# Attention with a learned bias and a gated MLP on one core: the bias hidden layer without a scale per row, and one more rounding on ScalarE

## The chip, the core and the metric

One core of a Trainium2 chip. The metric is the device time of one execution in microseconds (us). The time before is the median of three runs.

## The reference

Two stages, float32 in and out: attention over 4 batches, 8 heads, 576 positions and 64 columns a head, with a bias that a small network makes from the distance of two positions, and then an MLP of 512 to 2048 to 512 with the gate h * sigmoid(1.702 h).

```python
scores = scale * np.matmul(q, k.transpose(0, 1, 3, 2))
psi_rel = np.log1p(np.abs(rel))                                  # rel = i - j
psi_i = np.log1p(np.maximum(pos[:, None].astype(np.float32), 1.0))
x = (psi_rel / psi_i)[..., None]
h = np.maximum(x @ w1 + b1, 0.0)                                 # 32 hidden units
bias = h @ w2                                                    # 8 heads
scores = scores + bias.transpose(2, 0, 1)[None, :, :, :]
...
h = x @ w_in
g = h * (1.0 / (1.0 + np.exp(-1.702 * h)))
return (g @ w_out).astype(np.float32)
```

## The kernel before, in words

The queries are cut into five chunks of positions: four of 128 and one of 64. A unit is one batch, one chunk and one pair of heads. There are 72 units. For each, TensorE makes the scores (line 349), VectorE adds the bias and finds the row's extreme (L365), ScalarE takes the exponential and its sum (L369), and the probabilities are written as a rounded half-precision part (L381 on ScalarE, L379 on VectorE) and the rest of it (L382 on VectorE). A transposing DMA on SyncE's queue (L391) turns them, TensorE multiplies them with the values (L414), and VectorE writes the result as a high and a low half-precision part (L419, L420).

When the units of two batches in one chunk are done, they form a block of the MLP, of 256 tokens (128 for the last chunk). A block has 16 steps. In one step TensorE makes 128 hidden columns (L492), ScalarE takes the tanh (L498), VectorE makes the gate (L500), the gate is rounded to half precision (L505 on ScalarE for the blocks named in `ACT_G`, L507 on VectorE for the others), GpSimd takes the difference (L508), and TensorE multiplies high and low part with the second weight matrix two steps later (L522, `LAG = 2`). Both weight matrices come in 32 pieces; each is put together and split by four operations on VectorE (L456, L459, L462, L218) and one on ScalarE (L468).

The bias does not depend on the batch. It is made once, in 36 steps of 16 rows each, chunk by chunk (`bias_step`, or `bias_hidden` and `bias_products` as two halves). The 128 partitions hold four rows of 32 hidden units. `tab` holds the logarithm of the distance, 4 phases of 288 entries, and a window of 4 x 144 entries of it is the distance of 4 rows from all 576 columns. One step has four relus (line 163 on ScalarE or line 165 on VectorE, by the letters in `BIAS_ENG`: three on VectorE and one on ScalarE for each of the first 8 steps, all four on ScalarE in the next 16, two and two in the last 12), eight products on TensorE (L183, L185) into one PSUM buffer, an eviction on ScalarE (L189) and a store to a scratch tensor in DRAM (L190). The units load it from there (L204). The first 8 steps stand before the first unit, the others lie among the units.

The relus before multiply the window by `sc`, which is w1 divided by the logarithm of the row, with a scale for each partition. On ScalarE the bias b1 is added in the same operation. On VectorE the operation is a multiplication and a maximum with -b1, and the missing b1 times w2 is added where the products leave PSUM: `oc` holds this for each number of ScalarE relus in a step.

The library that builds the program orders the instructions of each engine itself: it goes by the order in which they are written as a priority, and by a planner's estimate of when each can start. Every engine then takes its own instructions strictly in that order.

Of the kernel before, what the change touches and what calls it, by code (L numbers as in the profile page):

```python
# [7 lines left out]
F32 = mybir.dt.float32  # L8
F16 = mybir.dt.float16
U32 = mybir.dt.uint32  # L10
ACTF = mybir.ActivationFunctionType
ALU = mybir.AluOpType
# [3 lines left out]
LPH = 288  # L16
PB0 = 144
# [3 lines left out]
def kernel(  # L21
# [26 lines left out]
    nc = tc.nc  # L48
    B, H, S, D = q.shape
# [22 lines left out]
    VEC_EXP = {u: 1 for u in (*range(33, 42), *range(62, 72))}  # L72
    VEC_EXP.update({u: 2 for u in (5, 6, 42, *range(54, 62))})
    POOL_W = set()
    ACT_G = {4, 6, 9}


    W_AHEAD = 3
# [7 lines left out]
    cst = ctx.enter_context(tc.tile_pool(name="cst", bufs=1))  # L86
# [9 lines left out]
    tab = cst.tile([128, 4, LPH], F32, name="tab")  # L96
    pk = cst.tile([128, 178], F32, name="pk")
    sc, w2b, w1c, b1c = pk[:, 0:144], pk[:, 144:176], pk[:, 176:177], pk[:, 177:178]
    b1n = cst.tile([128, 1], F32, name="b1n")
    oc = cst.tile([128, 5], F32, name="oc")  # L100
    scr = [dr.tile([128 if c < 4 else ST, H, S], F32, name=f"scr{c}") for c in range(5)]


# [15 lines left out]
    for g in range(B // 2):  # L119
        b0, b1_ = 2 * g, 2 * g + 1  # L120
        for c in range(5):
            n = 128 if c < 4 else ST
# [6 lines left out]


    def bias_setup():
        nc.scalar.activation(out=oc[:, 4:5], in_=oc[:, 4:5], func=ACTF.Relu)
        nc.vector.tensor_scalar(out=b1n, in0=b1c, scalar1=-1.0, scalar2=None, op0=ALU.mult)
        nc.vector.tensor_scalar(out=sc, in0=sc, scalar1=w1c, scalar2=None, op0=ALU.mult)
        nc.vector.tensor_scalar(out=w2b, in0=w2b, scalar1=BS, scalar2=None, op0=ALU.mult)
        p = ps_h.tile([128, 512], F32, tag="h", name="pc")
        for r in range(4):
            nc.tensor.matmul(p[32 * r:32 * r + 32, 0:1], lhsT=w2b, rhs=b1c, start=True, stop=True)
        for na in range(4):
            n = 32 * (4 - na)  # L140
            nc.vector.tensor_copy(oc[:n, na:na + 1], p[:n, 0:1])

    def bias_step(c, s, eng, htags, ostag):

        bias_products(c, s, eng, bias_hidden(c, s, eng, htags), ostag)

    def bias_hidden(c, s, eng, htags):
        hts = []
        na = eng.count("A")
        assert eng.endswith("A" * na)
        for r in range(4):
            if r % 2 == 0:
                ht = stage([128, 2, S], F32, htags[r // 2], "ht")
                hts.append(ht)
            h = ht[:, r % 2, :].rearrange("k (c p) -> k c p", c=4)
            pb, col = 32 * c + 4 * s + r, 32 * c + 4 * s + r  # L160
            tv = tab[:, :, PB0 - pb:PB0 - pb + 144]
            if eng[r] == "A":
                nc.scalar.activation(out=h, in_=tv, func=ACTF.Relu, bias=b1c, scale=sc[:, col:col + 1])  # L163
            else:
                nc.vector.tensor_scalar(  # L165
                    out=h, in0=tv, scalar1=sc[:, col:col + 1], scalar2=b1n, op0=ALU.mult, op1=ALU.max
                )
        return hts

    def bias_products(c, s, eng, hts, ostag):  # L170
        na = eng.count("A")
        where = BIAS_PSUM.get(8 * c + s)
        if where is None:
            o = ps_s.tile([128, 4, 512], F32, tag="s", name="o")[:, 0:2].rearrange("p a n -> p (a n)")
        else:
            o = ps_o.tile([128, 2, 512], F32, tag="o", name="o").rearrange("p a n -> p (a n)")
        om, ot = o[:, 0:SM], o[:, SM:S]
        for x in range(2):
            for r in range(4):
                h = hts[r // 2][:, r % 2, :].rearrange("k (c p) -> k c p", c=4)  # L180
                po = slice(32 * r, 32 * r + 32)
                if x == 0:
                    nc.tensor.matmul(om[po], lhsT=w2b, rhs=h[:, :, 0:128], start=True, stop=True)  # L183
                else:
                    nc.tensor.matmul(  # L185
                        ot[po], lhsT=w2b, rhs=h[:, :, 128:144].rearrange("k c p -> k p c"), start=True, stop=True
                    )
        os_ = wk.tile([128, S], F32, tag=ostag, name="os", bufs=BUFS[ostag])
        nc.scalar.activation(out=os_, in_=o[:, 0:S], func=ACTF.Identity, bias=oc[:, na:na + 1])  # L189
        nc.scalar.dma_start(out=scr[c][16 * s:16 * s + 16].rearrange("p h n -> (p h) n"), in_=os_)  # L190

    bt_t = {}
# [18 lines left out]
    def stage(shape, dt, tag, name):  # L211
        return wk.tile(shape, dt, tag=tag, name=name, bufs=BUFS[tag])
# [268 lines left out]
    def emit_m1(j, f):  # L481
# [21 lines left out]
        gt = wk.tile([128, 2, 256], F16, tag="gT", name="gT", bufs=BUFS["gT"])  # L503
        if j in ACT_G:
            nc.scalar.copy(gt[:, 0, :n], g[:, :n])  # L505
# [74 lines left out]
    for g in range(B // 2):  # L580
        b0, b1_ = 2 * g, 2 * g + 1
        o = g * UPG
# [15 lines left out]
            ):  # L598
                at(o + u, *x)

    nc.gpsimd.memset(oc, 0.0)
    nc.sync.dma_start(out=tab, in_=dist.rearrange("p (f a) -> p f a", a=LPH))
    nc.scalar.dma_start(out=pk, in_=pack)
    load_k(0, 0, "a32")
# [8 lines left out]
        out=idn, in_=idn, compare_op=ALU.not_equal, fill=1.0, base=0, pattern=[[-1, 128]], channel_multiplier=1  # L613
    )
    bias_setup()
    load_v(1, 0)
    load_k(0, 1)
    HT0 = ("ht", "hl", "ht", "aT")
    for s in range(8):
        bias_step(0, s, BIAS_ENG[s], (HT0[(2 * s) % 4], HT0[(2 * s + 1) % 4]), ("os", "bt")[s // 2 % 2])  # L620
        if s in FIRST:
            FIRST[s][0](*FIRST[s][1:])
    for x in SECOND:
        x[0](*x[1:])
    bq = [(c, i) for c in range(1, 5) for i in range(8 if c < 4 else 4)]
# [4 lines left out]
    def bias_first():  # L630
        if bq:
            c, i = bq.pop(0)
            eng = BIAS_ENG[8 * c + i]
            half.append((c, i, eng, bias_hidden(c, i, eng, ("ht", "ht"))))

    def bias_second():
        if half:
            x = half.pop(0)
            bias_products(*x, "os")
            bdone[x[0]] += 1  # L640
# [98 lines left out]
```

## Time and profile before

| | |
|---|---|
| median of 3 runs (lowest, highest) | 725.68 us (724.52, 728.96) |
| the profiled execution | 725.27 us, of which 723.5 us are the span from the first to the last instruction |
| TensorE matmul busy | 642.0 us, 89% of the span |
| VectorE busy | 514.7 us, 71% |
| ScalarE busy | 408.1 us, 56% |
| GpSimd busy | 133.9 us, 19% |
| mean granted TensorE clock | 0.959 of full speed |

The busy times are unions over the whole span. The span has two very different parts, and the shares of the whole describe neither. In the rows below PE is TensorE's matmul, PEld its weight load, DVE VectorE, ACT ScalarE, POOL GpSimd, and SPq, ACTq the instruction queues of SyncE and ScalarE. A number after L is a line of the kernel before. An operation's duration and the step from its start to the next one's start are not the same: neighbours on one engine overlap by some 0.1 us.

### The profile page before, as it was taken

What the parts mean: (1) busy time and instruction counts of PE and PEld (TensorE: products, weight loads), DVE (VectorE), ACT (ScalarE), POOL (GpSimd) and SP (SyncE); (2) the same over time, 40 slices, a digit from 0 to 9 for tenths busy, and PEclk for the clock granted to TensorE, in tenths of its full rate; (3) what the DMA queues carried; (4) which work ended last, traced back from release to release, by engine and by line L of the source; (5) the groups of instructions that cost most, each with busy time, mean ns of one, the idle gap of its engine ahead of it and who ended that gap; (6) DMA issues with size and microseconds to landing.
All of it is one profiled execution on the core that took longest, in us unless ns stands there. A gap on an engine that the chain in (4) does not pass through costs nothing. (4 is left out here: it accounts for less than half of the span.)

```text
span 723.5 us, 17516 instructions
## 1 busy us (share of the span) xinstructions
PE 642.0 (89%) x6888; PEld 385.0 (53%) x6888; DVE 514.7 (71%) x1416; ACT 408.1 (56%) x847; POOL 133.9 (19%) x194
## 2 busy tenths in 40 slices
PE   5655777869969999999979899899999999999997
PEld 3212333425536655656646465566666666666765
DVE  6865998798957766777677877855775896775321
ACT  6897978686558655665544446743443453343133
POOL 1202000111201111212221112121222222212222
PEclk9967978998989999999999999999999999999999
DMA  9889999968997656867576789955564475745000
GB/s 241 236 259 237 240 241 289 259 158 221 216 175 174 132 116 134 178 149 154 127 173 115 164 146 148 189 134 107 100 129 106 100 167 126 122 77 96 2 31 15
DMA packets 230771, 111.80 MB, mean 155 GB/s; under 512 B 210720, under 2 KB 214944, under 8 KB 230688
## 3 DMA queue, kind: packets, MB, share of 16 engines
q1 hardware_dynamic: 222592, 94.65, 62.7%
q10 hardware_dynamic: 7952, 15.43, 7.0%
q8 instruction: 54, 0.88, 0.5%
q0 software_dynamic: 144, 0.59, 0.2%
q14 instruction: 29, 0.24, 0.1%
HBM read 52.85 MB, written 15.34 MB: 94 GB/s over the span
## 5 line engine op out<-in xcount | busy, mean ns | idle before, releaser
L492 PE MATMUL hp<-xT,wi 128*128 128x256 f16 (+1 forms) x1920 | 216.9, 265 | 4.5 <-DVE th L500 3.6
L522 PE MATMUL op<-wo,gT 128*128 128x512 f16 x864 | 214.4, 381 | 4.9 <-DVE sm L376 2.4
L508 POOL TENSOR_TENSOR gT<-th,gT 128x256 f16<-128x256 f32 (+1 forms) x160 | 118.5, 742 | 513.0 <-DVE gT L507 279.9
L492 PEld LDWEIGHTS <-wi 128*128 128x128 f16 x1920 | 168.0, 98 | 48.5 <-issue 15.7
L369 ACT ACTIVATE a<-a,mx 128x576 f32<-128x576 f32 x144 | 110.4, 767 | 107.2 <-DVE mx L365 104.5
L382 DVE SCALAR_TENSOR_TENSOR hl<-a,sm,hl 128x576 f16<-128x576 f32 x144 | 121.7, 854 | 16.9 <-ACT hl L381 16.6
L365 DVE CUSTOM_DVE_ANT_0 a<-sp,bt 128x576 f32<-128x576 f32 x144 | 103.0, 752 | 35.5 <-PE sp L349 30.5
L522 PEld LDWEIGHTS <-gT 128*128 128x128 f16 x864 | 78.9, 98 | 84.1 <-POOL gT L508 5.1
L498 ACT ACTIVATE th<-hp 128x256 f32<-128x256 f32 (+1 forms) x160 | 56.4, 353 | 114.6 <-PE hp L492 109.6
L500 DVE SCALAR_TENSOR_TENSOR th<-th,hp 128x256 f32<-128x256 f32 (+1 forms) x160 | 62.2, 390 | 76.2 <-ACT th L498 76.0
L414 PE MATMUL ot<-aT,v 128*64 128x128 f16 (+1 forms) x2280 | 79.5, 221 | 26.8 <-DMA aT<-hl 25.2
L414 PEld LDWEIGHTS <-v 128*64 128x64 f16 x2400 | 69.5, 114 | 63.2 <-issue 43.1
L381 ACT ACTIVATE hl<-a,sm 128x576 f16<-128x576 f32 x103 | 76.3, 766 | 30.0 <-DVE sm L377 11.9
L183 PE MATMUL o<-ht,pk 128*32 128x512 f32 x288 | 69.6, 690 | 17.2 <-ACT os L189 13.8
L163 ACT ACTIVATE ht<-tab,pk 128x576 f32<-128x576 f32 x96 | 78.3, 860 | 9.3 <-PE o L185 5.0
L349 PE MATMUL sp<-kT,qT 64*128 64x512 f16 (+2 forms) x960 | 72.1, 292 | 8.2 <-DVE mx L365 5.9
L349 PEld LDWEIGHTS <-qT 64*128 64x128 f16 (+1 forms) x960 | 29.6, 98 | 56.9 <-issue 26.9
L419 DVE TENSOR_SCALAR xT<-ot 128x128 f16<-128x128 f32 x72 | 20.4, 284 | 22.1 <-PE ot L414 21.8
L507 DVE CAST gT<-th 128x256 f16<-128x256 f32 x112 | 32.6, 291 | 3.5
L376 DVE TENSOR_SCALAR sm<-sm 128x1 f32<-128x1 f32 x144 | 21.0, 149 | 16.2 <-ACT a L369 15.5
L189 ACT ACTIVATE os<-o,oc 128x576 f32<-128x576 f32 x36 | 26.3, 730 | 10.2 <-PE o L185 9.4
L165 DVE TENSOR_SCALAR ht<-tab,pk,b1n 128x576 f32<-128x576 f32 x48 | 26.9, 609 | 4.9 <-PE o L185 4.9
(57 smaller groups left out, 416.3 us busy)
## 6 DMA issues: line engine op xcount, KB each, us to landing
bt<-scr SPq DMA_DIRECT2D x31, 576.0 KB, 4.6
scr<-os ACTq DMA_DIRECT2D x36, 288.0 KB, 5.0
w<-in_moe_w_in_dram SPq DMA_DIRECT2D x16, 512.0 KB, 5.1
w<-in_moe_w_out_dram SPq DMA_DIRECT2D x16, 512.0 KB, 5.6
k<-in_k_dram SPq DMA_DIRECT2D x32, 128.0 KB, 3.9
q<-in_q_dram SPq DMA_DIRECT2D x16, 256.0 KB, 4.6
out_dram<-ob ACTq DMA_DIRECT2D x16, 256.0 KB, 3.0
bt<-scr SPq DMA_DIRECT2D x8, 288.0 KB, 4.1
```

The lines of the kernel that those rows point to most:

```text
L163: nc.scalar.activation(out=h, in_=tv, func=ACTF.Relu, bias=b1c, scale=sc[:, col:col + 1])
L183: nc.tensor.matmul(om[po], lhsT=w2b, rhs=h[:, :, 0:128], start=True, stop=True)
L349: nc.tensor.matmul(ps[a][64 * e:64 * e + m, cs], lhsT=qt[r, x, hp + e, 0:m], rhs=kT[b, hp + e][r, y, cs], start=i == 0, stop=i == 2,)
L365: nc.vector.tensor_tensor_reduce(out=at[:, cs], in0=s_ps.pop((u, a))[:, 0:S], in1=bt[:, cs], scale=-1.0 / BS, scalar=3.0e38, op0=ALU.add, ...
L369: nc.scalar.activation(out=at[:, cs], in_=at[:, cs], func=ACTF.Exp, scale=-1.0, bias=mx[:, a:a + 1], accum_out=sm[:, a:a + 1],)
L381: nc.scalar.activation(out=hl[:, 0, cs], in_=at[:, cs], func=ACTF.Identity, scale=r)
L382: nc.vector.scalar_tensor_tensor(out=hl[:, 1, cs], in0=at[:, cs], scalar=r, in1=hl[:, 0, cs], op0=ALU.mult, op1=ALU.subtract)
L414: nc.tensor.matmul(o[64 * a:64 * a + 64, po], lhsT=vt[:, x, vc:vc + 64], rhs=t[:, 9 * y + k0, po], start=kb < 0 and i == 0, stop=kb == 3 a ...
L492: nc.tensor.matmul(p[:, :n], lhsT=wi16[:, x, cc, 128 * f:128 * f + 128], rhs=r, start=i == 0, stop=i == 11,)
L500: nc.vector.scalar_tensor_tensor(out=g[:, :n], in0=th[:, :n], scalar=1.0, in1=p[:, :n], op0=ALU.add, op1=ALU.mult)
L508: nc.gpsimd.tensor_tensor(out=gt[:, 1, :n], in0=g[:, :n], in1=gt[:, 0, :n], op=ALU.subtract)
L522: nc.tensor.matmul(op_t[j, i], lhsT=gt[:, x, ts], rhs=wo16[:, f, y, :], start=f == 0 and n3 == 0, stop=f == NF - 1 and n3 == 2,)
```

## The change

The relus no longer multiply. The table is multiplied by w1 once, in place, and the bias of a row becomes b1 times the logarithm of the row (`bp`). As the logarithm is not negative, the relu of this is the old hidden value times that logarithm, and the division by it is done at the eviction with a scale for each partition (`ips`). A ScalarE relu has one per-partition operand (the bias) where it had two, a VectorE relu adds one per-partition operand and takes the maximum with a constant, where it had two per-partition operands. The eviction has a scale where it had a bias.

The setup is done in two parts by the new function `bias_scale`: what the first 8 steps need (32 columns of `bp`, table entries 112 to 287) before them, and the rest (112 columns, entries 0 to 111) after the last relus of these steps on their engines. `ips` is made by four products of the packed table with a matrix of ones (`one`, five small writes by GpSimd) and one copy. Besides this, `ACT_G` gets block 0, so the 16 gate roundings of the first MLP block move from VectorE (L507) to ScalarE (L505).

```diff
-    ACT_G = {4, 6, 9}
+    ACT_G = {0, 4, 6, 9}
...
     def bias_setup():
-        nc.scalar.activation(out=oc[:, 4:5], in_=oc[:, 4:5], func=ACTF.Relu)
-        nc.vector.tensor_scalar(out=b1n, in0=b1c, scalar1=-1.0, scalar2=None, op0=ALU.mult)
-        nc.vector.tensor_scalar(out=sc, in0=sc, scalar1=w1c, scalar2=None, op0=ALU.mult)
+        nc.scalar.activation(out=ips[:, 0:1], in_=one[:, 0:1], func=ACTF.Relu)
+        bias_scale(slice(0, 32), slice(PB0 - 32, LPH))
         nc.vector.tensor_scalar(out=w2b, in0=w2b, scalar1=BS, scalar2=None, op0=ALU.mult)
         p = ps_h.tile([128, 512], F32, tag="h", name="pc")
         for r in range(4):
-            nc.tensor.matmul(p[32 * r:32 * r + 32, 0:1], lhsT=w2b, rhs=b1c, start=True, stop=True)
-        for na in range(4):
-            n = 32 * (4 - na)
-            nc.vector.tensor_copy(oc[:n, na:na + 1], p[:n, 0:1])
+            nc.tensor.matmul(
+                p[32 * r:32 * r + 32, 0:36], lhsT=one, rhs=sc.rearrange("k (x r) -> k x r", r=4)[:, :, r],
+                start=True, stop=True,
+            )
+        nc.vector.tensor_copy(ips, p[:, 0:36])
+
+    def bias_scale(rows, dist):
+        nc.vector.reciprocal(out=bp[:, rows], in_=sc[:, rows])
+        nc.scalar.activation(out=tab[:, 2:4, dist], in_=tab[:, 2:4, dist], func=ACTF.Copy, scale=w1c)
+        nc.vector.tensor_scalar(out=bp[:, rows], in0=bp[:, rows], scalar1=b1c, scalar2=None, op0=ALU.mult)
+        nc.vector.tensor_scalar(
+            out=tab[:, 0:2, dist], in0=tab[:, 0:2, dist], scalar1=w1c, scalar2=None, op0=ALU.mult
+        )
...
             if eng[r] == "A":
-                nc.scalar.activation(out=h, in_=tv, func=ACTF.Relu, bias=b1c, scale=sc[:, col:col + 1])
+                last["A"] = nc.scalar.activation(out=h, in_=tv, func=ACTF.Relu, bias=bp[:, pb:pb + 1])
             else:
-                nc.vector.tensor_scalar(
-                    out=h, in0=tv, scalar1=sc[:, col:col + 1], scalar2=b1n, op0=ALU.mult, op1=ALU.max
+                last["V"] = nc.vector.tensor_scalar(
+                    out=h, in0=tv, scalar1=bp[:, pb:pb + 1], scalar2=0.0, op0=ALU.add, op1=ALU.max
                 )
...
-        nc.scalar.activation(out=os_, in_=o[:, 0:S], func=ACTF.Identity, bias=oc[:, na:na + 1])
+        nc.scalar.activation(out=os_, in_=o[:, 0:S], func=ACTF.Copy, scale=ips[:, 8 * c + s:8 * c + s + 1])
...
-    nc.gpsimd.memset(oc, 0.0)
+    nc.gpsimd.memset(one, 0.0)
+    for r in range(4):
+        nc.gpsimd.memset(one[32 * r:32 * r + 1, 8 * r:8 * r + 8], 1.0)
...
+    with tc.issue_after(last["V"].ins), tc.issue_after(last["A"].ins):
+        bias_scale(slice(32, 144), slice(0, PB0 - 32))
     for x in SECOND:
         x[0](*x[1:])
```

## Rows read from the trace of the kernel before

**Rows 1.** Busy time by stretch; columns: stretch, length, PE, PEld, DVE, ACT, POOL, clock, DMA, GB/s.

```profile
0.00:36.00 36.00, 21.35 (x203) 11.08 (x204) 25.89 (x52) 26.90 (x42) 8.32 (x21) 1.00 0.96 238
36.00:126.00 90.00, 61.73 (x542) 24.98 (x542) 72.34 (x186) 77.98 (x136) 4.71 (x5) 0.79 1.01 255
126.00:160.00 34.00, 28.46 (x255) 13.90 (x253) 28.50 (x67) 26.17 (x46) 6.81 (x6) 1.00 0.85 206
160.00:215.00 55.00, 41.91 (x422) 24.78 (x422) 45.48 (x117) 32.47 (x63) 7.62 (x8) 0.89 0.98 211
215.00:330.00 115.00, 112.98 (x1230) 68.11 (x1228) 84.48 (x242) 71.66 (x144) 19.86 (x27) 0.99 0.67 145
```

**Rows 2.** Waits of the first 135 us: who for whom, total us, times, longest us.

```profile
PE o L183 <- ACT os L189: 13.8, 9, 4.2
...
PE ot L414 <- DMA aT<-hl: 7.6, 3, 5.2
...
DVE a L365 <- DMA bt<-scr: 4.4, 2, 3.9
...
DVE wo L218 <- ACT wo L468: 3.2, 1, 3.2
```

**Rows 3.** Groups by line and shape: busy us, mean ns of one, idle before, releasers.

```profile
L163 ACT ACTIVATE ht<-tab,pk 128x576 f32<-128x576 f32 x96 | 78.3, 860 | 9.3 <-PE o L185 5.0 <-DVE pk L134 2.8 <-ACT ht L163 0.7
L381 ACT ACTIVATE hl<-a,sm 128x576 f16<-128x576 f32 x103 | 76.3, 766 | 30.0 <-DVE sm L377 11.9 <-issue 10.2 <-DMA aT<-hl 3.6
L165 DVE TENSOR_SCALAR ht<-tab,pk,b1n 128x576 f32<-128x576 f32 x48 | 26.9, 609 | 4.9 <-PE o L185 4.9
L189 ACT ACTIVATE os<-o,oc 128x576 f32<-128x576 f32 x36 | 26.3, 730 | 10.2 <-PE o L185 9.4 <-DMA out_dram<-ob 0.5
L507 DVE CAST gT<-th 128x256 f16<-128x256 f32 x112 | 32.6, 291 | 3.5
L377 DVE RECIPROCAL sm<-sm 128x1 f32<-128x1 f32 x144 | 21.9, 158 | 2.1
L379 DVE TENSOR_SCALAR hl<-a,sm 128x576 f16<-128x576 f32 x41 | 21.4, 527 | 0.7 <-DMA aT<-hl 0.2
L505 ACT CAST gT<-th 128x256 f16<-128x256 f32 x16 | 6.4, 397 | 4.1 <-DVE th L500 4.1
L134 DVE TENSOR_SCALAR pk<-pk 128x144 f32<-128x144 f32 x1 | 0.3, 285 | 0.0
```

**Rows 4.** Timeline, first 41 us: start, duration, what, idle before it and its releaser.

```profile
5.06 0.15 DVE L133 TENSOR_SCALAR b1n<-pk 128x1 f32<-128x1 f32 x1 [5.06 <-DMA pk<-in_pack_dram]
...
5.45 3.16 ACT L163 ACTIVATE ht<-tab,pk 128x576 f32<-128x576 f32 x4 [2.76 <-DVE pk L134]
...
14.57 1.56 DVE L165 TENSOR_SCALAR ht<-tab,pk,b1n 128x576 f32<-128x576 f32 x3 [1.92 <-PE o L185]
...
24.48 0.68 DVE L218 SCALAR_TENSOR_TENSOR qT<-qp,qT 128x512 f16<-128x512 f32 x1
...
29.48 0.72 ACT L189 ACTIVATE os<-o,oc 128x576 f32<-128x576 f32 x1
...
40.81 0.76 DVE L365 CUSTOM_DVE_ANT_0 a<-sp,bt 128x576 f32<-128x576 f32 x1 [3.93 <-DMA bt<-scr]
```

**Rows 5.** Stretches of line 163 alone: length, ACT busy and count, clock, DMA.

```profile
36.00:126.00 90.00, 34.65 (x43) 0.79 1.01 255
126.00:160.00 34.00, 13.08 (x16) 1.00 0.85 206
```

**Rows 6.** Stretches of line 507 alone: length, DVE busy and count, clock, DMA.

```profile
126.00:160.00 34.00, 1.71 (x6) 1.00 0.85 206
160.00:215.00 55.00, 2.22 (x8) 0.89 0.98 211
```

**Rows 7.** TensorE's timeline from 75 us, the product with the turned probabilities.

```profile
163.84 1.81 PE L414 MATMUL ot<-aT,v 128*64 128x128 f16 x30 [4.14 <-DMA aT<-hl]
```

**Rows 8.** Waits from 196 to 216 us, who for whom, total us, times, longest us.

```profile
PE ot L414 <- DMA aT<-hl: 5.6, 1, 5.6
```

More of the change, by code (lines that the diff above doesn't have):

```diff
@@ L98 @@
     sc, w2b, w1c, b1c = pk[:, 0:144], pk[:, 144:176], pk[:, 176:177], pk[:, 177:178]
-    b1n = cst.tile([128, 1], F32, name="b1n")
-    oc = cst.tile([128, 5], F32, name="oc")
+    bp = cst.tile([128, 144], F32, name="bp")
+    ips = cst.tile([128, 36], F32, name="ips")
+    one = cst.tile([128, 32], F32, name="one")
     scr = [dr.tile([128 if c < 4 else ST, H, S], F32, name=f"scr{c}") for c in range(5)]
@@ L137, in bias_setup @@
         for r in range(4):
-            nc.tensor.matmul(p[32 * r:32 * r + 32, 0:1], lhsT=w2b, rhs=b1c, start=True, stop=True)
-        for na in range(4):
-            n = 32 * (4 - na)
-            nc.vector.tensor_copy(oc[:n, na:na + 1], p[:n, 0:1])
+            nc.tensor.matmul(
[10 more added lines that the diff above has]
+        )
+    last = {}
     def bias_step(c, s, eng, htags, ostag):
@@ L152, in bias_hidden @@
         hts = []
-        na = eng.count("A")
-        assert eng.endswith("A" * na)
         for r in range(4):
@@ L159, in bias_hidden @@
             h = ht[:, r % 2, :].rearrange("k (c p) -> k c p", c=4)
-            pb, col = 32 * c + 4 * s + r, 32 * c + 4 * s + r
+            pb = 32 * c + 4 * s + r
             tv = tab[:, :, PB0 - pb:PB0 - pb + 144]
             if eng[r] == "A":
-                nc.scalar.activation(out=h, in_=tv, func=ACTF.Relu, bias=b1c, scale=sc[:, col:col + 1])
+                last["A"] = nc.scalar.activation(out=h, in_=tv, func=ACTF.Relu, bias=bp[:, pb:pb + 1])
             else:
-                nc.vector.tensor_scalar(
-                    out=h, in0=tv, scalar1=sc[:, col:col + 1], scalar2=b1n, op0=ALU.mult, op1=ALU.max
+                last["V"] = nc.vector.tensor_scalar(
+                    out=h, in0=tv, scalar1=bp[:, pb:pb + 1], scalar2=0.0, op0=ALU.add, op1=ALU.max
                 )
@@ L170, in bias_products @@
     def bias_products(c, s, eng, hts, ostag):
-        na = eng.count("A")
         where = BIAS_PSUM.get(8 * c + s)
```

## The prediction

> **What bounds the kernel now.** I read the busy times by stretch first [rows 1], since the whole says only that TensorE is busy for 642 of 723.5 us. From 215 to 330 us TensorE is busy for 112.98 of 115 us at a clock of 0.99, and the slices after it stay like that. What is saved on another engine there is hidden. The first 215 us are the part that can give: TensorE works for 21.35 + 61.73 + 28.46 + 41.91 = 153 us of them and is idle for 62. Between 36 and 126 us the two engines that carry the change are nearly full, VectorE with 72.34 and ScalarE with 77.98 of 90 us, the DMA engines show a share of 1.01, and the mean granted clock is 0.79, so part of it ran at 2.4 GHz and part at the lower level, with TensorE idle for 28 us in between. From 126 to 215 us VectorE has 28.50 + 45.48 = 74.0 of 89 us and ScalarE 58.6.
>
> Next come the waits, to see who is late in that part [rows 2]. TensorE waits 13.8 us for the eviction of the bias products (one PSUM buffer takes turns, so a product waits for ScalarE's eviction of the step before), and in single pieces of up to 5.2 us for transposed probabilities. VectorE waits 4.4 us for the bias loads and 3.2 us for ScalarE's part of a weight piece. TensorE's other two large holes are of the same kind, 4.14 us before the product at 163.84 [rows 7] and 5.6 us before the one at 211.6 [rows 8], both ended by a transposing DMA. So this part is a relay of VectorE, the SyncE queue with its transposes, and ScalarE. ScalarE is the fullest for 90 us, but it is rarely the last to arrive.
>
> **What one operation gives.** The groups by shape [rows 3] hold the same ScalarE form with one per-partition operand and with two, on 576 columns each: 766 ns at L381 and 860 ns at L163. The relu loses one operand, so I take 860 - 766 = 94 ns off each. On VectorE L379 has one such operand and takes 527 ns, L165 has two and takes 609 ns, so 82 ns go. L379 writes half precision and L165 does not, which makes this the weaker of the two. In all, 96 x 94 = 9.0 us of ScalarE and 48 x 82 = 3.9 us of VectorE. The evictions have one operand before and after and count as nothing, at most the 730 - 766 = 36 ns either way that separate two forms with one operand, 1.3 us over 36 off the path.
>
> **Part by part, against the profiled execution of 725.27 us** (2 us more than its span, and 0.41 us under the median of the three runs, which is inside their spread).
>
> Start, 0.3 us later. The packed inputs arrive at 5.06 us and the first relus start at 5.45 us on both engines [rows 4]. Now the table has to be multiplied in between: 352 columns on either engine. For 576 columns and one per-partition operand ScalarE takes 766 ns [rows 3]. If that were all proportional, 352 columns would take 766 x 352 / 576 = 468 ns, and if none of it were, 766, so I take about 0.6 us. The table is then ready near 5.7 us. The bound below is -0.6 us (the 8 relus that VectorE runs first give back 0.7 us and nothing else comes later), above +0.6.
>
> The first 8 steps, nothing. VectorE runs ahead by the two buffers and then waits 1.92 us for the products to let go of them [rows 4], so its 24 faster relus (2.0 us) end in a longer wait. The ScalarE relus save 8 x 94 ns = 0.75 us where it waits too.
>
> Second part of the setup, 0.7 us later. It stands in the program ahead of the query transposes of the second batch, on VectorE behind the last relu of step 7. In this trace the subtraction of that transpose starts there at 24.48 us [rows 4]. Queued behind the new operations are that subtraction, then the key transposes on TensorE, the products of step 7, the eviction at 29.48 us, its store, and the bias load that ends VectorE's wait of 3.93 us at 40.81 us. Two multiplications cost about 285 ns (L134, 144 columns) and between 285 and 527 ns for 224 columns, so 0.33. The reciprocal of 112 columns shows only its one-column time, 158 ns, in this trace. The bound above is the 285 ns of a 144-column operation from the rows, doubled for a slower operation. That is 0.75 to 1.2 us in durations, some 0.2 less in starts, and I take 0.7. Below it is 0, if the planner puts the subtraction first, above 1.2.
>
> The reciprocal is the one operation whose growth with the columns no row shows, since all 144 of them have one column and take 158 ns [rows 3]. The Trainium skill, VectorE: DVE Perf Modes, section First, the fixed hardware budget, says that a reciprocal is an iterated division with a repeat count of 8. An estimate from that page, 8 cycles a column at 0.96 GHz, is 0.93 us for the 112 columns, and the sum would be 0.7 us higher by it.
>
> ScalarE relus among the units, 0.8 us earlier. Between 36 and 126 us there are 43 of them and 16 more up to 160 us [rows 5]. 59 x 94 ns = 5.5 us is the most. Of the waits of other engines in the first 135 us, 13.8 us on the evictions and 3.2 us on a weight part end on ScalarE [rows 2], against a stretch of about 100 us with units in it. That is one us in six, and 5.5 / 6 = 0.9, of which I take 0.8. Below the bound is -5.5, above 0.
>
> The gate roundings of block 0, 1.5 us earlier. Fourteen of the 16 lie between 126 and 215 us [rows 6]. VectorE loses 16 x 291 ns = 4.7 us [rows 3]. It is busy for 83% of the stretch [rows 1], but three long holes there end on DMAs [rows 7, 8], so I let a third pass. ScalarE gains 16 x 397 ns = 6.4 us [rows 3] and has 89 - 58.6 = 30 us free in the stretch. The move adds a wait. In the block that has this form already ScalarE stood 4.1 us before 16 roundings until VectorE's gate was ready [rows 3], 0.26 us each. Behind it in ScalarE's order stand the next tanh, exponentials and evictions, and for those wait TensorE and VectorE. I count it at nothing, because the free 30 us hide 6.4 + 4.1 us, and because two steps lie between the rounding and the product. With that cover gone it costs 16 x (0.397 - 0.291 + 0.26) = 5.9 us. The bounds are -4.7 and +5.9.
>
> The last 24 relus on each engine lie at 160 us and later, mostly under a full TensorE. Nothing, at most -0.3 us for the eight pairs before 215 us.
>
> Ones and products of the setup: five small GpSimd writes before the transposes need it, four products with 36 columns instead of one, one copy for four. Nothing.
>
> Sum: 0.3 + 0.7 - 0.8 - 1.5 = -1.3 us, so 724.0 us.
>
> **Rivals.**
> 1. ScalarE paces the first part after all. For it: 77.98 of 90 us busy [rows 1], and the eviction is TensorE's largest wait [rows 2]. Against it: the holes that end on DMAs. Then the 5.5 us of relus and the 4.7 us of VectorE's roundings come through, and 725.27 + 1.0 - 5.5 - 4.7 gives 716.1 us. Chance 0.17.
> 2. The rounding on ScalarE holds up what stands behind it. For it: ScalarE takes its instructions in order, and block 0 falls where relus, exponentials and weight pieces are all still on it, while the one block of 256 tokens that has the form now comes in the second half. Against it: 30 us free. It decides where VectorE is late with the gate, and it is 83% busy in this stretch. Full price 5.9 us in place of the 1.5 saved: 725.27 + 1.0 - 0.8 + 5.9 = 731.4 us. Chance 0.13.
> 3. Another order. The planner has new durations and a new setup in the middle, and the three transposes with holes of 5.2, 4.14 and 5.6 us [rows 2, 7, 8] may land better or worse. One hole more or less is 5 us: 719 or 729 us, half each. Chance 0.17.
> 4. The change doesn't do what it says: the relus keep 860 and 609 ns, because a maximum with a constant and an addition cost as much. Then 725.27 + 1.0 - 1.5 = 724.8 us. Chance 0.03.
>
> **How the numbers follow.** The forecast of 724.0 us has the remaining chance of 0.50, with a range of its own from 720.5 to 727.5 us. A change under 1% (7.3 us) can't be told from none here. Faster than 718.4 us needs rival 1 nearly whole (0.14) or a lucky order on top of the forecast (0.05), so 0.19. Slower than 733.0 us needs rival 2 on top of a bad order, 0.09. The rest is 0.72. Leaving out the lower part of rival 1 and the upper part of rivals 2 and 3 gives 716 to 731 us for 8 of 10.
>
> **What would show it.** Right: L163's successor at about 766 ns and L165's at about 527, the first relu near 5.8 us, the first bias load landing no earlier than 40.8 us, L505's successor with 16 more of 256 columns, and the stretch from 215 us on unchanged and only shifted by a us or two. TensorE would still have three holes of 4 to 6 us that end on transposes. Rival 1 shows in a stretch of 36 to 126 us that is some 5 us shorter. Rival 2 shows in exponentials that start late behind an idle of the roundings. What would make the number wrong is a step of which this trace has no row: the order that the planner writes.

## The result and the profile after

| | before | after |
|---|---|---|
| median (lowest, highest) | 725.2 us (724.52, 728.96), 4 runs | 717.21 us (715.95, 718.13), 4 runs |
| the profiled execution, its span | 725.27 us, 723.5 us | 715.95 us, 714.2 us |
| mean granted TensorE clock | 0.959 | 0.956 |

After to before is 0.9864, 95% interval [0.9827, 0.9902]. The medians differ by 8.0 us, a ratio of 0.9890, which lies inside the interval; 1.3 us less was forecast. The ratios count only the runs within 1.5% of the fastest of their kernel, which in one experiment below, `early_transpose_then_free`, are five of twelve.

First the page of the kernel after, busy time by engine.

```profile
PE 637.2 (89%) x6888; PEld 385.7 (54%) x6888; DVE 510.9 (72%) x1401; ACT 404.4 (57%) x865; POOL 135.5 (19%) x198
```

ScalarE is busy for 3.7 us less and VectorE for 3.8. TensorE has 4.8 us less, with the same 6888 products. The rest of the 9.3 us by which the span is shorter, 4.5 us, is idle time that TensorE no longer has.

Busy time by stretch of the kernel after, columns as in [rows 1].

```profile
0.00:36.00 36.00, 21.61 (x202) 10.68 (x202) 23.30 (x51) 25.22 (x42) 8.22 (x25) 0.95 0.92 231
36.00:126.00 90.00, 62.31 (x580) 27.52 (x581) 75.79 (x190) 79.16 (x145) 4.98 (x6) 0.81 1.03 257
126.00:160.00 34.00, 28.27 (x293) 15.78 (x290) 32.24 (x78) 28.34 (x57) 4.44 (x6) 0.95 0.99 267
160.00:215.00 55.00, 45.55 (x486) 25.75 (x485) 44.96 (x110) 37.05 (x76) 10.49 (x11) 0.94 0.93 197
215.00:330.00 115.00, 114.92 (x1262) 71.34 (x1257) 87.34 (x250) 68.39 (x143) 23.96 (x30) 1.00 0.73 151
```

Against [rows 1] the counts of products tell more than the shares. By 215 us TensorE has issued 202 + 580 + 293 + 486 = 1561 of them where the kernel before had 203 + 542 + 255 + 422 = 1422 (one that crosses a border counts twice, a few on either side). The work of the first part is done earlier, and up to 215 us the granted clock is lower in two of the stretches (0.95 for 1.00) and higher in two (0.81 for 0.79, 0.94 for 0.89). Most of the gain lies where the prediction said that one could lie, ahead of 215 us. It is six times as large.

Groups by line and shape of the kernel after, columns as in [rows 3].

```profile
L172 ACT ACTIVATE ht<-tab,bp 128x576 f32<-128x576 f32 x96 | 69.3, 768 | 6.5 <-PE o L193 5.7 <-ACT ob L540 0.4 <-DVE ips L142 0.3
L197 ACT ACTIVATE os<-o,ips 128x576 f32<-128x576 f32 x36 | 26.3, 731 | 12.1 <-PE o L193 11.5 <-DMA out_dram<-ob 0.6
L174 DVE TENSOR_SCALAR ht<-tab,bp 128x576 f32<-128x576 f32 x48 | 23.0, 532 | 3.0 <-PE o L193 2.8
L513 ACT CAST gT<-th 128x256 f16<-128x256 f32 x32 | 12.6, 397 | 7.2 <-DVE th L508 7.1
L145 DVE RECIPROCAL bp<-pk 128x112 f32<-128x112 f32 x1 | 0.8, 845 | 0.0
L145 DVE RECIPROCAL bp<-pk 128x32 f32<-128x32 f32 x1 | 0.4, 353 | 5.2 <-DMA pk<-in_pack_dram 5.2
```

The operations cost what the prediction read for them: 768 and 532 ns for the relus (forecast 766 and 527), 731 ns for the eviction (730 before), and 7.2 us of waits ahead of 32 roundings, 0.22 us each (0.26 forecast). Only the reciprocal was off, with 845 ns for 112 columns where 570 was the upper bound taken.

Two of TensorE's groups of products, in the kernel before and then in the kernel after: columns as in [rows 3].

```profile
L183 PE MATMUL o<-ht,pk 128*32 128x512 f32 x288 | 69.6, 690 | 17.2 <-ACT os L189 13.8 <-DVE mx L365 2.3 <-ACT ht L163 0.8
L414 PE MATMUL ot<-aT,v 128*64 128x128 f16 x1800 | 69.2, 226 | 23.7 <-DMA aT<-hl 22.1 <-DVE xT L420 1.5
```

```profile
L191 PE MATMUL o<-ht,pk 128*32 128x512 f32 x288 | 63.0, 693 | 20.9 <-ACT os L197 18.2 <-DVE mx L373 1.7 <-DVE ht L174 1.0
L422 PE MATMUL ot<-aT,v 128*64 128x128 f16 x1800 | 69.4, 227 | 14.0 <-DMA aT<-hl 10.1 <-DVE sm L384 2.5 <-DVE w L470 1.4
```

Ahead of the product with the turned probabilities the wait for the transposing DMA has fallen from 22.1 to 10.1 us in the form shown. The wait for the eviction on ScalarE, the one that faster relus should have shortened, has grown from 13.8 to 18.2. And the bias products cover 6.6 us less of the span although one of them takes 690 and 693 ns: more of them lie beside each other. These waits do not explain the gain, because they move as far in profiles of kernels that are no faster. TensorE's waits for transposes over all forms of that product (total us, times, longest us), in the kernel before, in the kernel after and in `early_transpose_old_order`, and last its wait for the evictions in `cheap_relu_old_order`; the two experiments follow below, and their time is that of before:

```profile
PE ot L414 <- DMA aT<-hl: 25.2, 11, 5.6
...
PE ot L422 <- DMA aT<-hl: 15.3, 6, 5.6
...
PE ot L422 <- DMA wo<-hl: 4.3, 1, 4.3
...
PE ot L414 <- DMA aT<-hl: 14.5, 8, 6.9
PE ot L414 <- DMA wo<-hl: 6.1, 1, 6.1
...
PE o L183 <- ACT os L189: 18.4, 11, 3.9
```

The waits for transposes are 25.2, then 15.3 + 4.3 = 19.6, then 14.5 + 6.1 = 20.6 us, and the last of the three kernels gains nothing. The wait for the evictions grows to 18.4 us in the order of before as well.

That the order is another shows most plainly at the first unit's probabilities. Timeline of the kernel before from 53 us.

```profile
53.91 3.72 SPq L391 DMA_TRANSPOSE aT<-hl  x1
...
63.04 1.81 PE L414 MATMUL ot<-aT,v 128*64 128x128 f16 x30 [5.22 <-DMA aT<-hl]
...
64.89 0.29 DVE L419 TENSOR_SCALAR xT<-ot 128x128 f16<-128x128 f32 x1 [4.53 <-PE ot L414]
...
65.68 1.14 POOL L225 TENSOR_SCALAR v<-v 128x1152 f32<-128x1152 f32 x1 [30.28 <-DVE sm L376]
...
66.86 1.29 ACT L330 ACTIVATE v<-v 64x128 f16<-64x128 f32 x3 [3.88 <-POOL v L225]
...
69.22 0.78 DVE L218 SCALAR_TENSOR_TENSOR wo<-w,wo 128x512 f16<-128x512 f32 x1 [3.21 <-ACT wo L468]
...
74.15 0.75 DVE L365 CUSTOM_DVE_ANT_0 a<-sp,bt 128x576 f32<-128x576 f32 x1
```

And of the kernel after, from 49 us.

```profile
49.51 3.96 SPq L399 DMA_TRANSPOSE aT<-hl  x1
...
57.52 0.43 PE L422 MATMUL ot<-aT,v 128*64 128x128 f16 x4
...
62.78 0.27 DVE L427 TENSOR_SCALAR xT<-ot 128x128 f16<-128x128 f32 x1
...
64.70 1.29 ACT L338 ACTIVATE v<-v 64x128 f16<-64x128 f32 x3 [0.33 <-POOL v L233]
...
65.42 0.76 DVE L373 CUSTOM_DVE_ANT_0 a<-sp,bt 128x576 f32<-128x576 f32 x1
...
73.49 2.59 PE L191 MATMUL o<-ht,pk 128*32 128x512 f32 x7 [4.94 <-ACT os L197]
```

Before, a chain of four engines stands still one after the other: TensorE 5.22 us for the transpose, VectorE 4.53 for TensorE's product, ScalarE 3.88 for a step of GpSimd that waits for VectorE, and VectorE 3.21 for ScalarE. After, the transpose is issued 4.4 us earlier, the product has no wait, and the chain is gone. A hole of 4.94 us appears behind it, ahead of the bias products. The softmax of the fifth unit begins 8.7 us earlier. This is more than the lead itself, since the new order also puts that softmax ahead of other work. By the end of the units the lead is 9.4 us, about the difference of the spans.

### The profile page after: what moved, and what is told of

Its sections match the earlier page's. It is cut to its first block, busy times and chain, and to the rows that moved or that the text cites. A ratio compares the mean times of both kernels' runs of the same rounds, so it can differ in the third digit from the quotient of the medians.

```text
span 714.2 us, 17518 instructions
## 1 busy us (share of the span) xinstructions
PE 637.2 (89%) x6888; PEld 385.7 (54%) x6888; DVE 510.9 (72%) x1401; ACT 404.4 (57%) x865; POOL 135.5 (19%) x198
## 5 line engine op out<-in xcount | busy, mean ns | idle before, releaser
L422 PE MATMUL ot<-aT,v 128*64 128x128 f16 (+1 forms) x2280 | 79.8, 222 | 19.2 <-DMA aT<-hl 15.3
L191 PE MATMUL o<-ht,pk 128*32 128x512 f32 x288 | 63.0, 693 | 20.9 <-ACT os L197 18.2
L172 ACT ACTIVATE ht<-tab,bp 128x576 f32<-128x576 f32 x96 | 69.3, 768 | 6.5 <-PE o L193 5.7
L197 ACT ACTIVATE os<-o,ips 128x576 f32<-128x576 f32 x36 | 26.3, 731 | 12.1 <-PE o L193 11.5
L191 PEld LDWEIGHTS o<-ht,pk 128*32 128x32 f32 x288 | 10.2, 115 | 40.9 <-ACT os L197 21.1
L515 DVE CAST gT<-th 128x256 f16<-128x256 f32 x96 | 28.1, 293 | 3.6
```

The costliest lines, as they stand in the source:

```text
L172: last["A"] = nc.scalar.activation(out=h, in_=tv, func=ACTF.Relu, bias=bp[:, pb:pb + 1])
L422: nc.tensor.matmul(o[64 * a:64 * a + 64, po], lhsT=vt[:, x, vc:vc + 64], rhs=t[:, 9 * y + k0, po], start=kb < 0 and i == 0, stop=kb == 3 a ...
```

## The experiments

All were timed in five rounds, in three groups, each against the kernel before on the same chip (medians of before 726.8, 727.77 and 726.55 us, of 29, 35 and 30 runs).

The first question is which of the two edits did it.

**`bias_alone`**: the kernel after without the moved rounding.

```diff
-    ACT_G = {0, 4, 6, 9}
+    ACT_G = {4, 6, 9}
```

> The kernel after without block 0 in the set of blocks rounded on ScalarE, so the bias part alone, ordered by the planner as it likes. If the bias part carries the 8.0 us (cheaper relus, or the order that the planner makes of them): 717 to 719.5 us. If the moved rounding carries it: 723 to 726 us. My own sum of before would give 725.3 + 0.3 + 0.7 - 0.8 = 725.5 us.

Measured: 718.24 us, 0.9888 [0.9837, 0.9938].

**`gate_alone`**: the kernel before with the moved rounding.

```diff
-    ACT_G = {4, 6, 9}
+    ACT_G = {0, 4, 6, 9}
```

> The kernel before with block 0 rounded on ScalarE, nothing else. The orders of the engines are those of before up to the first gate of block 0, near 126 us. If VectorE's 16 roundings carry a good part: 719 to 722 us. By my sum: -1.5 us, about 724. If the rounding holds up ScalarE's queue: 727 to 731 us.

Measured: 728.71 us, 1.0024 [0.9994, 1.0054]. The bias part carries the gain. The rounding alone is no gain here. Its median lies in the range expected for a queue held up, but before ran 1.6 us slower in this group than in the result, and the interval includes 1.

The bias part has cheaper operations and, since the library's planner reckons with their prices, another order. These were separated by writing an order down and holding it: a dependency without a wait between each two neighbours of an engine.

```diff
+def _keep_order(nc, tc):
...
+    how = mybir.DependencyInfo(mybir.DependencyClass.NoSync, mybir.DependencyReason.DATA)
+    for steps in code.values():
...
+        for a, b in zip(names, names[1:]):
+            tc.add_manual_dep(known[b], a, how, reason="a given order")
```

The order is kept in the traces: in `cheap_relu_old_order` below, VectorE, GpSimd and SyncE's queue have the sequence of before from start to end. No run holds the order of before and changes nothing else, so the cost of holding is not measured by itself. The nearest is `early_transpose_old_order`, with the old operations and three of them moved, at 0.9996.

**`bias_old_order`**: `bias_alone`, with this function, and the instructions that it shares with the kernel before in the order of before on every engine.

> The bias part alone, with the instructions that it shares with the kernel before held to the order of before on every engine (edges that fix the order only, without a wait). The new setup instructions are placed freely. It separates the price of the relus from the planner's order. If the prices carry the gain (ScalarE paces): 717 to 720 us. If the order that the planner writes carries it: 724 to 726 us, since the setup costs 1 us more and the relus give back about as much.

Measured: 725.6 us, 0.9998 [0.9968, 1.0027].

**`old_price_new_order`**: the kernel after in its own order, held, with relus that have a second per-partition operand again (this makes the bias another than the reference's).

```diff
-                last["A"] = nc.scalar.activation(out=h, in_=tv, func=ACTF.Relu, bias=bp[:, pb:pb + 1])
+                last["A"] = nc.scalar.activation(out=h, in_=tv, func=ACTF.Relu, bias=bp[:, pb:pb + 1], scale=w1c)
...
-                    out=h, in0=tv, scalar1=bp[:, pb:pb + 1], scalar2=0.0, op0=ALU.add, op1=ALU.max
+                    out=h, in0=tv, scalar1=bp[:, pb:pb + 1], scalar2=b1c, op0=ALU.add, op1=ALU.max
```

> The kernel after in its own order on every engine, held by the same kind of edges, but each relu with a second per-partition operand again: ScalarE multiplies by w1 once more, VectorE compares with b1 in place of zero, so the bias values are others. If the order carries the gain: 717 to 720 us. If the prices carry it: 722 to 726 us, and the relus last 860 and 609 ns again.

Measured: 722.21 us, 0.9934 [0.9904, 0.9965]. Its groups by line show that the relus do have the old price:

```profile
L172 ACT ACTIVATE ht<-tab,bp,pk 128x576 f32<-128x576 f32 x96 | 78.2, 860 | 5.5 <-PE o L193 4.7 <-ACT ob L540 0.4 <-DVE ips L142 0.3
L174 DVE TENSOR_SCALAR ht<-tab,bp,pk 128x576 f32<-128x576 f32 x48 | 26.6, 609 | 2.1 <-PE o L193 2.0
```

The time lies in the range expected from the prices. But before ran at 726.8 us in this group, and 0.9934 of the 725.2 us of the result is 720.4 us, between the two ranges. So the cheap operations in the old order give nothing, and the new order with dear operations is faster than before, by 0.7% or 4.8 us. From 0.9934 to 0.9864 the cheap operations then give another 0.7%, 5 us (with the two intervals, between about 1.6 and 8.6 us). By the medians (722.21 / 726.8 = 0.9937 and 0.9890) it is 3.4 us, and the kernel after has four runs, from another occasion. So this second half is the less certain one.

The second group asks how far this holds. **`cheap_relu_old_order`**: the kernel before in its own order, held, only the relus made cheaper, without setup (the bias is another).

```diff
-                nc.scalar.activation(out=h, in_=tv, func=ACTF.Relu, bias=b1c, scale=sc[:, col:col + 1])
+                nc.scalar.activation(out=h, in_=tv, func=ACTF.Relu, bias=b1c)
...
-                    out=h, in0=tv, scalar1=sc[:, col:col + 1], scalar2=b1n, op0=ALU.mult, op1=ALU.max
+                    out=h, in0=tv, scalar1=sc[:, col:col + 1], scalar2=0.0, op0=ALU.mult, op1=ALU.max
```

> The kernel before in its own order, with one per-partition operand in each relu: ScalarE leaves out the scale, VectorE compares with zero in place of -b1, so the bias values are others. No setup is added. It takes the setup's 1 us apart from the relus' gain. By my sum (a sixth of the saving arrives): 724 to 725.5 us. If ScalarE paces the first part: 717 to 720 us.

Measured: 726.69 us, 0.9997 [0.996, 1.0035]. The time is above both ranges, but before itself ran at 727.77 us in this group. By the ratio the relus give nothing here, and 0.4% at most by the interval.

**`whole_old_order`**: the whole change, shared instructions in the order of before, the 16 moved roundings and the setup where the planner puts them between these.

> The whole change with all instructions that it shares with the kernel before held to the order of before; the setup and the 16 moved roundings are placed freely. If the planner's order carries the gain: 723.5 to 726.5 us, as with the bias part alone in that order. If the roundings of block 0 give what I counted: 722.5 to 724.5 us. By rival 1 716 us.

Measured: 724.33 us, 0.9961 [0.9928, 0.9994]. The forecast of -1.3 us is 0.9982 and lies inside. The time is in the first two ranges, which overlap, so it does not tell what the roundings give.

**`old_until_unit4`** and **`old_from_unit4`**: `bias_alone` in the order of before up to the softmax of the fifth unit and free from there, and the reverse.

> The bias part alone (717 to 719 us with the planner's own order, 725.6 us in the order of before). Here each engine is held to the order of before until the softmax of the fifth unit (near 74 us there), and the planner is free after that. If the gain lies in the order of the first units, where the first transposed probabilities come 5 us earlier: 723 to 726 us. If it lies in what comes later: 717 to 720 us.

> The bias part alone, the other half: the planner is free until the softmax of the fifth unit, and each engine is held to the order of before from there to the end. If the gain lies in the order of the first units and is kept: 717 to 720 us. If the later order makes it, or gives it back: 722 to 727 us.

Measured: 725.2 us, 0.9958 [0.9929, 0.9988], for `old_until_unit4`, and 727.86 us, 1.0001 [0.9972, 1.0031], for `old_from_unit4`. Timeline of `old_from_unit4`, the softmax of the fifth and of the sixth unit:

```profile
66.12 0.76 DVE L373 CUSTOM_DVE_ANT_0 a<-sp,bt 128x576 f32<-128x576 f32 x1
...
74.93 0.69 DVE L226 SCALAR_TENSOR_TENSOR kT<-kp,kT 128x512 f16<-128x512 f32 x1 [2.12 <-ACT kT L302]
...
76.65 0.76 DVE L373 CUSTOM_DVE_ANT_0 a<-sp,bt 128x576 f32<-128x576 f32 x1
```

The lead at the fifth unit is 8.0 us (66.12 against 74.15), at the sixth 2.7 (76.65 against 79.33). Between the two VectorE is idle for 2.12 us in one piece and for the rest does the work that the new order had left behind the softmax. At the seventh 1 us of lead is left, and none at the end. Neither half of the new order brings the 8 us alone: the free later half gives 0.4%, 3 us, the free first half nothing (its time is just above the second range expected).

The third group asks what starts the lead and what makes the planner write the new order. **`early_transpose_old_order`**: the kernel before in its own order, held, with three instructions moved forward around the first unit (no code differs but the list that `_keep_order` reads). **`early_transpose_then_free`**: the same, held only up to the second transposing DMA.

> The kernel before in its own order, with three instructions moved: the second rounding of the first unit on ScalarE goes ahead of the two exponentials that stood before it, its difference on VectorE directly behind the first one's, and the first transposing DMA ahead of the load of queries and the three loads of values that stood before it on SyncE's queue. If the place of the first transpose is what starts the lead, the softmax of the fifth unit begins at 66 to 71 us and not at 74.15; and as the later order of before gave such a lead back, the time is 724 to 728 us, ratio 0.997 to 1.002. If the first transpose alone is enough: 717 to 721 us, ratio 0.986 to 0.993. If the lead at the fifth unit comes from elsewhere, the softmax stays at 73 to 75 us.

> The kernel before, its order held with the same three moves up to the second transposing DMA, and left to the planner from there, with the old operations. If any order that follows a lead at the fifth unit keeps some of it: 718 to 723 us, ratio 0.988 to 0.995. If the planner's order with the old prices gives the lead back as the old one does: 724 to 729 us, ratio 0.997 to 1.003.

Timeline of `early_transpose_old_order`:

```profile
50.44 2.81 SPq L391 DMA_TRANSPOSE aT<-hl  x1
...
58.75 1.20 PE L414 MATMUL ot<-aT,v 128*64 128x128 f16 x30
...
66.51 0.77 DVE L218 SCALAR_TENSOR_TENSOR wo<-w,wo 128x512 f16<-128x512 f32 x1 [2.14 <-ACT wo L468]
...
71.42 0.75 DVE L365 CUSTOM_DVE_ANT_0 a<-sp,bt 128x576 f32<-128x576 f32 x1
```

The product comes 4.3 us earlier and without a wait, so the place of the transpose is the cause of that hole. At the softmax of the fifth unit 2.7 us of it are left, just short of the range expected, because in the old order VectorE still has a weight part that waits for ScalarE and four differences ahead of it. The time is 726.82 us, 0.9996 [0.9967, 1.0025]: nothing. The second kernel ran from 715.01 to 727.97 us, with a median of 725.9 us and a ratio of 0.9925 [0.9885, 0.9965]. The mean of all twelve is 0.3% under that of before. By its median it is before's equal, by its fastest run it is as fast as the kernel after. I conclude nothing from it, and so it stays open whether the planner can write as good an order with the old prices.

**`cheap_relu_free_order`**: the diff of `cheap_relu_old_order`, the order left to the planner. **`dear_relu_new_setup`**: the diff of `old_price_new_order`, the order left to the planner.

> The kernel before with the cheaper relus alone (ScalarE without its scale, VectorE's maximum with 0.0 in place of -b1, so the bias is another than the reference's), no setup, no moved rounding, and the order left to the planner. The same operations in the order of before gave a ratio of 0.9997. If it is the price of an operation that makes the planner write another and better order: 717 to 721 us, ratio 0.985 to 0.992. If the order came from the new setup in the middle, or from the moved rounding, the planner's new order here is only another one and gives 724 to 729 us, ratio 0.997 to 1.003.

> The kernel after with relus of the old price (a second per-partition operand on each engine, so the bias is another than the reference's), order left to the planner, which now counts the dear relus. If the price makes the better order, this loses it: 723 to 728 us, ratio 0.995 to 1.003, and slower than the 722.2 us of the same operations in the order of the kernel after. If the setup in the middle or the moved rounding makes it: 718 to 722.5 us, ratio 0.988 to 0.994.

Measured: 721.23 us, 0.9927 [0.9897, 0.9956], just above the range expected from the price, and 725.5 us, 0.9992 [0.9966, 1.0018]. So the cheaper relus alone are enough for a better order here, and the setup and the rounding with dear relus are not. In the first of them the old chain is cut at the same place:

```profile
52.30 3.94 SPq L391 DMA_TRANSPOSE aT<-hl  x1
...
59.03 1.03 PE L414 MATMUL ot<-aT,v 128*64 128x128 f16 x30 [0.32 <-DMA aT<-hl]
...
69.12 0.75 DVE L365 CUSTOM_DVE_ANT_0 a<-sp,bt 128x576 f32<-128x576 f32 x1
```

But this is not what makes an order better. In `dear_relu_new_setup`, which gains nothing, the softmax of the fifth unit begins 5.2 us earlier than before too:

```profile
68.97 0.76 DVE L373 CUSTOM_DVE_ANT_0 a<-sp,bt 128x576 f32<-128x576 f32 x1
```

The ratios to before of the kernels with one order throughout, by what the operations are and whose order they stand in (the intervals are above, 0.3 to 0.5% to each side):

| operations | order of before | the planner's own | order of after |
|---|---|---|---|
| cheap relus, no setup | 0.9997 | 0.9927 | |
| bias part | 0.9998 | 0.9888 | |
| bias part and rounding | 0.9961 | 0.9864 | 0.9864 |
| rounding alone | | 1.0024 | |
| setup and rounding, dear relus | | 0.9992 | 0.9934 |

## Why the prediction was wrong

The step that failed is the one under the sum: every term was worked out on the order of before, and "another order" stood beside it as rival 3, as one hole more or less, 5 us, with even odds and a chance of 0.17. The runs put the order in the middle. In the column of before's order the ratios are 0.9961 to 0.9998, and the sum of -1.3 us (0.9982) fits them. In the planner's own order the same operations give 0.9864 to 0.9927. The order is worth 0.7% even with the old prices (0.9934), and the prices, worth nothing in the old order, give about as much again in the new one, though less surely. The time of 717.21 us is inside the range of 716 to 731, near its edge, and there rival 1 stood with its 716.1 for another reason. So it is luck that the range holds it. What came, a better order on top of the forecast, stood in the prediction with a chance of 0.05.

**Prices.** Right, within 5 ns for the relus, so rival 4 falls. The reciprocal was too cheap: 845 ns for 112 columns and 353 for 32, 6.2 ns a column. The Trainium skill, VectorE: DVE Perf Modes, section First, the fixed hardware budget, gives the repeat count of 8 from which the prediction worked out an estimate of 0.93 us for the first; the measured 0.85 us is nearer to that than to the 0.57 us which the prediction took as its upper end.

**Start, +0.3 us.** Half of what came, which is just beyond the bound of +0.6. Timeline of the kernel after:

```profile
5.17 0.35 DVE L145 RECIPROCAL bp<-pk 128x32 f32<-128x32 f32 x1 [5.17 <-DMA pk<-in_pack_dram]
...
6.09 6.23 DVE L174 TENSOR_SCALAR ht<-tab,bp 128x576 f32<-128x576 f32 x14
...
17.88 0.84 DVE L145 RECIPROCAL bp<-pk 128x112 f32<-128x112 f32 x1
...
23.14 0.68 DVE L226 SCALAR_TENSOR_TENSOR qT<-qp,qT 128x512 f16<-128x512 f32 x1
...
29.10 1.36 DVE L226 SCALAR_TENSOR_TENSOR kT<-kp,kT 128x1152 f16<-128x1152 f32 x1 [5.28 <-ACT kT L284]
...
41.51 0.76 DVE L373 CUSTOM_DVE_ANT_0 a<-sp,bt 128x576 f32<-128x576 f32 x1 [3.30 <-DMA bt<-scr]
```

The first relus start at 6.09 us against 5.45 [rows 4], +0.64. The prediction watched ScalarE's multiplication of the table. What came last was VectorE's row of five small operations, from 5.17 to 6.08 us.

**Second part of the setup, +0.7 us.** The size was met, by another way. VectorE's three operations took 845 + 238 + 266 ns = 1.35 us, more than the 0.75 to 1.2 us that were summed. The first softmax is 0.70 us later here (41.51 against 40.81) and 0.75 in `bias_old_order`. But the query subtraction, behind which the prediction saw everything queued, starts at 23.14 us where it was 24.48, and at 24.47 in `bias_old_order`: the work ahead of it has become shorter by as much as the setup takes on VectorE, or more. What is late in the kernel after is the key piece that VectorE waits 5.28 us for from ScalarE (29.10 against 28.05 us), whose queue now holds the table's second multiplication and, in the new order, casts of the values ahead of it.

**ScalarE relus, -0.8 us (bounds -5.5 and 0).** Right in the old order, where setup and relus together come to nothing (0.9998) and the relus alone to 0.9997. Rival 1, ScalarE as the pace, is refuted there. In the new order the cheap operations of both engines are worth about 5 us, near the bound. In that order TensorE's wait for the evictions is 21.3 us with the dear relus and 18.2 with the cheap ones. The bias products of `old_price_new_order`:

```profile
L191 PE MATMUL o<-ht,pk 128*32 128x512 f32 x288 | 64.9, 690 | 24.8 <-ACT os L197 21.3 <-DVE mx L373 2.2 <-DVE ht L174 1.1
```

This suggests that ScalarE's work lies partly on the path there, but it is read from one profile each and not shown. "One us in six" was read from waits that belong to the old order.

**Gate roundings, -1.5 us.** Not settled. From 0.9998 to 0.9961 in the old order is -2.7 us, from 0.9888 to 0.9864 in the new one -1.7, and alone it is +1.7 us in an order of its own. All pairs of intervals overlap or touch. Rival 2, a price of 5.9 us, is refuted (the upper end of `gate_alone` is 1.0054, 3.9 us), and the waits of 0.22 us ahead of each rounding are there; whether they are hidden is not shown. The prediction let a third pass because of three long holes that end on DMAs, but in the stretch that it named its rows show two, both on TensorE.

**Three holes of 4 to 6 us at transposes.** There are three again, though the order is another:

```profile
107.03 1.81 PE L422 MATMUL ot<-aT,v 128*64 128x128 f16 x30 [3.93 <-DMA aT<-hl]
...
115.21 1.81 PE L422 MATMUL ot<-wo,v 128*64 128x128 f16 x30 [4.30 <-DMA wo<-hl]
...
198.11 1.81 PE L422 MATMUL ot<-aT,v 128*64 128x128 f16 x30 [5.64 <-DMA aT<-hl]
```

Those before the products at 63.04 and 163.84 us are gone, two have come, and the last is as long as the one of 5.6 us before. So this sign was met and says nothing of the forecast.

**From 215 us on, unchanged and only shifted by a us or two.** The shift is 9.4 us at the end of the units, and TensorE is busy for 114.92 of 115 us in that stretch where it was for 112.98.

**What stays open.** Why the planner's order is better for the smaller price. The three free orders with cheap relus gave 0.9927, 0.9888 and 0.9864, the two with dear relus 0.9992 and 1.0024, and before is a third one, which looks like more than luck, but it is six orders. No single instruction explains it: the first transpose is where the new order shows first, and moving it gave nothing. Nor is it shown which waits in the new order make its 0.7%.

## What to carry to other kernels

Where a library orders the instructions by estimated prices, a change of 0.1 us in an operation is two changes, a price and a new order. Here the price gave nothing without the new order, and the new order gave about half of the gain without the price. Work the sum out on the old order, and then ask for the order as a term of its own: which waits between engines would change, and what the saved work is worth once they have. Nothing here foretells the sign of that term, so it belongs into the range. To learn afterwards which it was, hold the old order and run the new operations in it, and the reverse. A milestone that comes earlier isn't yet a lead, because the new order may only have put it ahead of other work, and a wait that shrinks is not yet time gained.

## What the runs showed of the hardware

The reciprocal on VectorE grows by 6.2 ns a column (353 ns at 32, 845 at 112), while the multiplication behind it in the setup (L147, one per-partition operand) takes 238 ns for 32 columns and 266 for 112:

```profile
L147 DVE TENSOR_SCALAR bp<-bp,pk x2: 238/252/266, 5.7 to 20.5; 128x32 f32<-128x32 f32 x1, 128x112 f32<-128x112 f32 x1
```

One kernel's executions differ by more than the forecast change: before ran from 722.51 to 731.78 us over 30 runs of one group. In the profile of `cheap_relu_old_order`, in the order of before throughout, the units from the 31st to the 37th took 3.7 us longer than in the profile of before. A single profile therefore can't price an order of instructions to better than some 4 us, and the leads above are of single profiles.
